# Where a small transpose's copy stands in a step, and which bank takes the last bias columns

## The chip, the cores and the metric

The kernel runs on one core of a Trainium2 chip. Its engines work side by side, each through its own queue in order: TensorE (PE, with PEld for its weight loads) multiplies matrices, VectorE (DVE) and ScalarE (ACT) work on elements and read TensorE's results out of PSUM, GpSimd (POOL) works on elements in SBUF, and SyncE (SP) issues the transfers between DRAM and SBUF. Engines wait for one another by semaphores. The metric is the time of one execution on the device, in microseconds. A profile is one execution with a record of each instruction; its span runs from the first instruction to the last.

## The reference, cut to what matters

Attention over 2 batches, 8 heads, 576 positions and 64 dimensions a head has a bias that a small network computes from the distance of two positions. Two feed-forward layers follow it.

```
scores = q @ k.T / sqrt(64)                      # per batch and head, 576 x 576
x      = log1p(|i - j|) / log1p(max(i, 1))       # distance seen from query position i
bias   = relu(x @ w1 + b1) @ w2                  # 1 -> 32 -> 8 heads
attn   = softmax(scores + bias) ;  y = attn @ v  # 1152 rows of 512
h      = y @ w_in ;  y2 = (h * clip(h + 3, 0, 6) / 6) @ w_out      # 512 -> 2048 -> 512
out    = ((y2 @ w_a) * (y2 @ w_b)) @ w_out2                        # 512 -> 1536 -> 512
```

For a fixed position i the bias depends only on |i - j|, so there are at most 576 distances for each i, and a row of the bias is a row of distances read forward and, for the keys before i, reversed.

## The kernel before, in words

**Steps.** The attention stage is a loop of 36 steps, n = 0 to 35 (line 426). A step handles a tile of 128 queries and a pair of heads u = 0, 1. The scores (L299) are 12 matmuls in three groups of four: K and Q are split into a high and a low part, and each group adds one product. They land in two PSUM tiles `sc` of two banks, one tile for each head of the pair; each bank holds 288 keys, so columns 288 to 511 of every bank stay free. On DVE one reduction a head (L304) adds the bias row, and keeps the minimum of the negated row; ACT takes the exponential with its sum (L308). DVE makes the denominators and their reciprocals (L312, L316), and POOL scales the probabilities (L321).

**Transposes.** Probabilities `P` are transposed one step later. The 64 tail keys of both heads, 128 columns in all, go first (L331), into free columns of the first bank of this step's first score tile, and DVE copies them out (L332). The other 1024 columns take eight transposes (L341) into two banks `tp`; ACT copies the first bank (L343), DVE the second (L345). Yet a step later the product with V follows (L359 for the tail keys, L363), into `pvb`, which is split into a high part (ACT, L372) and a low one (DVE, L378). The next step's scores go into the same two `sc` tiles again, so they wait until the reductions and the copy of the tail keys have read them. From step 27 on the tail keys' transpose uses a bank of its own (`tpb`), and ACT copies it.

**Bias.** While step n runs, it also prepares the bias of a slice g = n + 10 of 16 query positions, up to slice 35 in step 25. Four relus make the hidden layer for g + 1 (`bias_relu`: j = 0, 1, 2 on DVE at L194, j = 3 on ACT at L196). Four matmuls with 32 output rows each (L210) turn that for g into 8 heads of bias over the distances, in one PSUM bank `bps` that exists once. These are copied into an SBUF row `E`, forward and reversed (L216, L218, L225, L227), and SyncE writes E to a DRAM scratch (L239). Eight slices make a block of 128 query positions, which is loaded back as the bias tile of later steps (L259). A slice has 304 to 576 distances. Up to 512 fit one bank; above that, in steps 22 to 25, the distances are halved, and both halves pass through `bps` one after the other.

**Order.** The schedule is written out by hand: each engine runs its instructions in the order of the code, and the framework adds the semaphore waits. In steps 22 to 25 `bias_parts` is a generator that stops between the halves, so that the first half's matmuls stand right behind the scores and its copies ahead of the relus.

**After the steps** come the feed-forward layers, with `_Weights` preparing the weights. Their first three loads (L935) are issued in step 27, behind the last bias loads in SyncE's queue; from step 28 on POOL rescales the first weights (L946) between its normalisations.

Of the kernel before, what the change touches and what calls it, by code (L numbers as in the profile page):

```python
# [8 lines left out]
F32 = mybir.dt.float32  # L9
F32R = mybir.dt.float32r  # L10
AF = mybir.ActivationFunctionType
ALU = mybir.AluOpType
# [9 lines left out]
NSET = S // 16  # L22
NSTEP = 36
LEAD = 2
# [26 lines left out]
def kernel(ctx, tc, cons, qm, qt, kt, vm, vt, wm, out):  # L51
# [8 lines left out]
    V, A, G, T, SP = nc.vector, nc.scalar, nc.gpsimd, nc.tensor, nc.sync  # L60
# [10 lines left out]
    ps = tc.alloc_tile_pool(name="ps", bufs=1, space=PSUM, side="right", reuse_waits="tile")  # L71
    psc0 = tc.alloc_tile_pool(name="psc0", bufs=1, space=PSUM, side="left", reuse_waits="tile")
# [12 lines left out]
    cst3 = ph.tile([128, 1], F32, name="cst3")  # L85
    RELU = "VVVA"
# [45 lines left out]
    sc_tiles = {}  # L132
# [44 lines left out]
    def bias_geom(s):  # L177
        i0 = 16 * s
        R = i0 + 15
        return i0, R, max(R, S - 1 - i0) + 1  # L180

    def bias_relu(s, only=None):

        i0, R, Dd = bias_geom(s)
        if s not in h_tiles:
            h_tiles[s] = [ph.tile([128, S], F32, tag="h", bufs=8, name="ht") for _ in range(4)]
        for j in range(4):
            kind = RELU[j]
            if only is not None and kind not in only:
                continue  # L190
            ht = h_tiles[s][j]
            sc = scl[:, 4 * s + j : 4 * s + j + 1]
            if kind == "V":
                V.tensor_scalar(ht[:, :Dd], ltab[:, :Dd], scalar1=sc, scalar2=negb, op0=ALU.mult, op1=ALU.max)  # L194
            else:
                A.activation(ht[:, :Dd], ltab[:, :Dd], AF.Relu, bias=b1c, scale=sc)  # L196

    def bias_parts(s, rev, wide=False):

        i0, R, Dd = bias_geom(s)  # L200
        hs = h_tiles.pop(s)
        n = 1 if Dd <= 512 else 2
        step = Dd // n
        E = ph.tile([128, S + 16], F32, tag="E", bufs=4, name="E")

        def mm(c):
            bp = psc0.tile([128, 512], F32, tag="w", bufs=4, name="bpw") if wide else ps.tile([128, 512], F32, tag="b", name="bps")
            d0, d1 = c * step, Dd if c == n - 1 else (c + 1) * step
            for j in range(4):
                T.matmul(bp[32 * j : 32 * j + 32, : d1 - d0], w2b, hs[j][:, d0:d1], start=True, stop=True)  # L210
            return bp, d0, d1

        def leave(c, bp, d0, d1):
            f1 = min(d1, S - i0)
            if f1 > d0 and not wide and n > 1 and c == 0:
                V.tensor_scalar(E[:, R + d0 : R + f1], bp[:, : f1 - d0], scalar1=8.0, scalar2=cst3[:, 0:1], op0=ALU.mult, op1=ALU.add)  # L216
            elif f1 > d0:
                A.activation(E[:, R + d0 : R + f1], bp[:, : f1 - d0], AF.Identity, bias=cst3[:, 0:1], scale=8.0)  # L218
            r0, r1 = max(d0, 1), min(d1, R + 1)
            if r1 > r0:  # L220
                src = bp[:, r0 - d0 : r1 - d0]
                dst = E[:, R - r1 + 1 : R - r0 + 1]
                dst = bass.AP(dst.tensor, dst.offset + (r1 - r0 - 1), [dst.ap[0], [-1, r1 - r0]])
                if rev is A and (wide or n == 1 or c):
                    A.activation(dst, src, AF.Identity, bias=cst3[:, 0:1], scale=8.0)  # L225
                else:
                    V.tensor_scalar(dst, src, scalar1=8.0, scalar2=cst3[:, 0:1], op0=ALU.mult, op1=ALU.add)  # L227

        if wide:
            for x in [mm(c) for c in range(n)]:  # L230
                leave(0, *x)
        else:
            for c in range(n):
                leave(c, *mm(c))
                if c < n - 1:
                    yield
        it, sl = divmod(s, 8)
        scr = scratch[it]
        SP.dma_start(  # L239
            bass.AP(scr.tensor, scr.offset + PAD + 16 * sl * H * PITCH - 15, [[H * PITCH + 1, 16], [PITCH, H], [1, S + 15]]),  # L240
            E[:, : S + 15],
        )

    def bias_mm(*args, **kwargs):
        for _ in bias_parts(*args, **kwargs):
            pass

    def bias_load(it, half, pairs=None):
        scr = scratch[it]
# [17 lines left out]
    def qk_units(n):  # L267
        tl, p = divmod(n, 4)
        it = tl // 2
        P = pb.tile([128, 2, S], F32, tag="P", bufs=3, name="P")  # L270
        P_tiles[n] = P
        st = pb.tile([128, 4], F32, tag="st", bufs=4, name="st")
        st_tiles[n] = st


        scs = [psc.tile([128, 2, 512], F32, tag="sc", bufs=2, name="sc") for _ in range(2)]
        sc_tiles[n] = scs[0]
        if tl < 8:
            (qh, ql), j = q_tiles[n], 4 * (tl % 2) + p
            mm = [  # L280
                (u, c, slice(0, 128), q_, k_[:, j], x)
                for x, (q_, k_) in enumerate(((qh, KH), (qh, KL), (ql, KH)))
                for c in range(2)
                for u in range(2)
            ]
            last = 2
        else:

            mm = [
                (u, c, slice(64 * b, 64 * b + 64), q_raw[8][:, p], k_[:, 4 * b + p].bitcast(F32), x)  # L290
                for c in range(2)
                for x, k_ in enumerate((KH, KL))
                for b in range(2)
                for u in range(2)
            ]
            last = 1
        for u, c, r, q_, k_, x in mm:
            d = slice(64 * u, 64 * u + 64)
            T.matmul(scs[u][r, c, 0:288], q_[d, r], k_[d, 288 * c : 288 * c + 288], start=x == 0, stop=x == last)  # L299
        for u in range(2):  # L300
            h, sc = 2 * p + u, scs[u]
            bt = bias_tiles[it, p // 2][:, h % 4, :].rearrange("p (c x) -> p c x", c=2)
            Pu = P[:, u, :].rearrange("p (c x) -> p c x", c=2)
            V.tensor_tensor_reduce(  # L304
                out=Pu, in0=sc[:, :, 0:288], in1=bt, scale=-0.125, scalar=3.0e38,
                op0=ALU.add, op1=ALU.min, accum_out=st[:, u : u + 1],
            )
            A.activation(P[:, u, :], P[:, u, :], AF.Exp, bias=st[:, u : u + 1], scale=-1.0, accum_out=st[:, 2 + u : 3 + u])  # L308

    def denominators(n):  # L310
        st = st_tiles[n]
        V.tensor_scalar(st[:, 2:4], st[:, 2:4], scalar1=1e-9, scalar2=None, op0=ALU.add)  # L312
# [10 lines left out]
    def transpose_tail(n):  # L323

        PT_tiles[n] = pb.tile([128, 9, 128], F32, tag="PT", bufs=2, name="PT")
        if n < NSET - 8 - LEAD:

            tp = sc_tiles[n + 1][:, 0, 288 : 288 + 128]
        else:
            tp = ps.tile([128, 512], F32, tag="b", name="tpb")[:, 0:128]  # L330
        T.transpose(tp, P_tiles[n].rearrange("p a n -> p (a n)")[:, 512:640], ident)  # L331
        (V.tensor_copy if n < NSET - 8 - LEAD else A.copy)(PT_tiles[n][:, 8, :], tp)  # L332
# [56 lines left out]
    for s in range(8 + LEAD):  # L389
        if s < 7 + LEAD:  # L390
            bias_relu(s + 1)
        bias_mm(s, V, wide=True)
        if s in (1, 3):
            load_k(2 + s // 2)
        elif s == 5:
            k_hi(1, A)
        elif s == 6:
            k_lo(1, V)
        elif s == 7:
            load_k(4)  # L400
            load_k(5)
            q_hi(0)
        elif s == 8:
            bias_load(0, 0, 0)
            bias_load(0, 0, 1)
            k_hi(0, V)
            q_lo(0)
            k_lo(0, V)
# [17 lines left out]
    for n in range(NSTEP):  # L426
        g = n + 8 + LEAD
# [2 lines left out]
        if n + 2 < 32:  # L430
            q_hi(n + 2)
        qk_units(n)
        rest = bias_parts(g, A) if g < NSET else iter(())
        if g < NSET and bias_geom(g)[2] > 512:
            next(rest)
        if g + 1 < NSET:
            bias_relu(g + 1, only="V")
        if n >= 2:
            pv(n - 2)
            x_hi(n - 2)  # L440
        if n >= 1 and n - 1 >= NSET - 8 - LEAD:
            transpose_tail(n - 1)
        if g + 1 < NSET:
            bias_relu(g + 1, only="A")
        if g < NSET:
            for _ in rest:
                pass
            if g == NSET - 1:
                bias_load(g // 8, 0)
            elif g % 8 == 7:  # L450
                bias_load(g // 8, 0)
# [14 lines left out]
        if n >= NSTEP - 7:  # L466

            ring.join_next()
        denominators(n)
        reciprocals(n)  # L470
        normalise(n)
# [2 lines left out]
        if n + 2 < 32:  # L474
            q_lo(n + 2, G)
        if n >= 1:
            if n - 1 < NSET - 8 - LEAD:
                transpose_tail(n - 1)
            transposes(n - 1)
        if n >= NSTEP - 8:  # L480
            ring.join_next()
# [217 lines left out]
    for ch in range(NCH1):  # L699
        for i in range(3 if ch == 0 else 0, FC):  # L700
            w = first[i] if ch == 0 else ring.take()
# [456 lines left out]
```

## Time and profile before

| | before |
|---|---|
| median of 3 runs | 610.77 us (610.57 to 611.08) |
| profiled execution, whole | 610.01 us |
| its span | 608.2 us |
| PE busy | 591.7 us (97%) |
| DVE busy | 447.2 us (74%) |
| ACT busy | 341.9 us (56%) |
| POOL busy | 228.3 us (38%) |
| granted TensorE clock, mean | 0.994 of full speed |

Busy shares are averages over the whole span. The attention steps take about 28 to 185 us of it, and DVE is busy for close to nine tenths of most of their slices; behind them PE is full. A busy PE can include time in which a matmul that has been started waits for its PSUM tile, so the gaps between PE's groups are read from its weight loads (PEld) and from the timeline. "Idle before, and what ended it" stands in brackets behind a row, where the profile could tell.

### The profile page before, as it was taken

The page shows a single profiled execution, that of the slowest core. Times are in us where ns is not written, and L with a number is a line of the kernel's source. Part 1 is how long each engine was busy: PE and PEld are TensorE (multiplying, and loading weights), DVE is VectorE, ACT ScalarE, POOL GpSimd, SP SyncE. Part 2 cuts the span into 40 slices and gives each one's busy share as a digit, 9 for nine tenths or more (in the row PEclk, how much of TensorE's full clock was granted, in tenths as well). Part 3 has the DMA queues.
Part 4 walks back from the last instruction along what each step waited for, and adds up shares of the span by engine and source line. Part 5 has one row for each costly group of instructions (what it writes and reads, how often), then busy time and mean ns, then how long its engine had stood idle before and what let it go on. Part 6 is the DMA issues. An engine that isn't in the chain of part 4 may idle for free. (4 is left out here: it accounts for less than half of the span.)

```text
span 608.2 us, 13366 instructions
## 1 busy us (share of the span) xinstructions
PE 591.7 (97%) x5306; PEld 521.3 (86%) x5306; DVE 447.2 (74%) x909; ACT 341.9 (56%) x721; POOL 228.3 (38%) x224
## 2 busy tenths in 40 slices
PE   8699999998999999999999999999999999999997
PEld 5267776766778999999999999999989998899986
DVE  6899888887668993897796566968585577947252
ACT  6689888876877754652572353455446543345310
POOL 0055443434665421221212142365326834377200
PEclk9979999999999999999999999999999999999999
DMA  7874727255923444345333211011154212510012
GB/s 252 265 251 134 254 70 247 80 161 164 250 72 107 134 141 140 105 132 146 104 110 110 66 63 36 0 34 37 36 168 144 71 36 65 171 43 1 0 60 96
DMA packets 28877, 69.27 MB, mean 114 GB/s; under 512 B 5392, under 2 KB 5776, under 8 KB 28816
## 3 DMA queue, kind: packets, MB, share of 16 engines
q1 hardware_dynamic: 28672, 68.35, 37.1%
q8 instruction: 41, 0.67, 0.5%
q14 instruction: 20, 0.16, 0.1%
q10 hardware_dynamic: 144, 0.09, 0.0%
HBM read 55.17 MB, written 13.25 MB: 113 GB/s over the span
## 5 line engine op out<-in xcount | busy, mean ns | idle before, releaser
L980 POOL TENSOR_TENSOR slot<-wv,slot 128x512 fp32r<-128x512 f32 x86 | 118.7, 1385 | 220.3 <-ACT slot L979 156.5
L532 PE MATMUL pair<-xx,slot 128*128 128x384 f32 x576 | 101.5, 335 | 0.0
L532 PEld LDWEIGHTS pair<-xx,slot 128*128 128x128 f32 x576 | 99.8, 188 | 0.2
L532 PE MATMUL pair<-gh,slot 128*128 128x384 f32 x384 | 98.6, 336 | 0.0
L321 POOL TENSOR_SCALAR P<-P,st 128x576 f32<-128x576 f32 x72 | 57.1, 806 | 109.1 <-DVE xx L378 71.9
L740 PE MATMUL pair<-xx,slot 128*128 128x288 f32 x576 | 83.2, 296 | 0.5 <-DVE c L774 0.3
L740 PEld LDWEIGHTS pair<-xx,slot 128*128 128x128 f32 x576 | 78.6, 188 | 1.4 <-DVE c L774 0.6
L948 ACT ACTIVATE wv<-raw 128x512 f32<-128x512 f32 x63 | 42.5, 675 | 57.3 <-DMA raw<-in_wm_dram 34.4
L308 ACT ACTIVATE P<-P,st 128x576 f32<-128x576 f32 x72 | 55.3, 769 | 30.5 <-DVE st L304 30.5
L532 PEld LDWEIGHTS pair<-gh,slot 128*128 128x128 f32 x384 | 69.4, 188 | 0.0
L532 PE MATMUL pair<-slot,gh 128*128 128x512 f32 (+1 forms) x224 | 68.1, 387 | 0.0
L304 DVE CUSTOM_DVE_ANT_0 P<-sc,bias 128x576 f32<-128x576 f32 x72 | 51.7, 754 | 19.2 <-PE sc L299 13.0
L532 PE MATMUL pair<-gl,slot 128*128 128x384 f32 x192 | 64.6, 336 | 0.8 <-DVE gl L550 0.8
L740 PE MATMUL pair<-tt,slot 128*128 128x288 f32 x432 | 64.2, 298 | 0.9 <-ACT u L826 0.9
L979 ACT CAST slot<-wv 128x512 fp32r<-128x512 f32 x86 | 53.0, 620 | 18.9 <-PE pair L740 12.8
L740 PEld LDWEIGHTS pair<-tt,slot 128*128 128x128 f32 x432 | 59.1, 188 | 2.7 <-ACT u L826 2.0
L557 ACT ACTIVATE t<-pair,three 128x384 f32<-128x384 f32 x48 | 27.9, 582 | 45.4 <-PE pair L532 45.3
L532 PEld LDWEIGHTS pair<-slot,gh 128*128 128x128 f32 x224 | 41.3, 188 | 8.9 <-DVE part L883 0.3
L194 DVE TENSOR_SCALAR ht<-cs,scl,negb 128x576 f32<-128x576 f32 (+17 forms) x108 | 48.5, 504 | 0.0
L558 DVE SCALAR_TENSOR_TENSOR u<-t,pair 128x384 f32<-128x384 f32 x48 | 26.4, 550 | 24.7 <-ACT t L557 24.4
L957 DVE TENSOR_SCALAR wm<-wv 128x512 uint32<-128x512 uint32 x59 | 40.5, 686 | 4.8 <-ACT wv L948 4.7
L963 DVE SCALAR_TENSOR_TENSOR wv<-raw,wm 128x512 uint32<-128x512 uint32 x59 | 40.5, 686 | 4.0
(111 smaller groups left out, 1012.9 us busy)
## 6 DMA issues: line engine op xcount, KB each, us to landing
raw<-in_wm_dram SPq DMA_DIRECT2D x68, 512.0 KB, 3.6
scr<-E SPq DMA_DIRECT2D x36, 295.5 KB, 3.6
bias<-scr SPq DMA_DIRECT2D x7, 576.0 KB, 4.8
bias<-scr SPq DMA_DIRECT2D x7, 512.0 KB, 5.5
kraw<-in_kt_dram SPq DMA_DIRECT2D x8, 288.0 KB, 4.5
qraw<-in_qm_dram SPq DMA_DIRECT2D x8, 256.0 KB, 4.8
VM<-in_vm_dram SPq DMA_DIRECT2D x2, 1024.0 KB, 6.2
out_dram<-part SPq DMA_DIRECT2D x7, 256.0 KB, 2.0
```

What stands on the lines that cost most here:

```text
L194: V.tensor_scalar(ht[:, :Dd], ltab[:, :Dd], scalar1=sc, scalar2=negb, op0=ALU.mult, op1=ALU.max)
L304: V.tensor_tensor_reduce(out=Pu, in0=sc[:, :, 0:288], in1=bt, scale=-0.125, scalar=3.0e38, op0=ALU.add, op1=ALU.min, accum_out=st[:, u : u ...
L308: A.activation(P[:, u, :], P[:, u, :], AF.Exp, bias=st[:, u : u + 1], scale=-1.0, accum_out=st[:, 2 + u : 3 + u])
L321: G.tensor_scalar(P[:, u, :], P[:, u, :], scalar1=st[:, 2 + u : 3 + u], scalar2=1.0, op0=ALU.mult, op1=ALU.mult)
L532: T.matmul(ps_ap, l, r, start=(i == 0), stop=(i == len(prods) - 1))
L557: A.activation(t, hp, AF.Relu, bias=three[:, 0:1])
L740: T.matmul(pair[:, j, 0:TQ], l, r, start=start and i == 0, stop=i == 5, skip_group_check=not start)
L948: self.nc.scalar.mul(self.u[k], up, 2.0**-112)
L957: V.tensor_scalar(mid, ub, scalar1=3, scalar2=0x7FFFFFFF, op0=ALU.logical_shift_left, op1=ALU.bitwise_and)
L963: V.scalar_tensor_tensor(out=v, in0=self.words(k, 0), scalar=29, in1=mid, op0=ALU.logical_shift_right, op1=ALU.bitwise_or)
L979: nc.scalar.copy(s[:, 0, :], v)
L980: nc.gpsimd.tensor_tensor(out=s[:, 1, :], in0=v, in1=s[:, 0, :].bitcast(F32), op=ALU.subtract)
```

## The change

There are two edits. First, the tail keys' transpose and copy (`transpose_tail`) of steps 1 to 26 are called ahead of the third DVE relu, which itself is now called just ahead of the denominators, and no longer behind the POOL normalisation and the low parts. Second, `bias_mm` replaces the generator: in steps 22 to 25 the first 512 distances go into `bps`, and those from 512 on into the second bank of this step's second score tile, from column 288. All bias matmuls of a step now stand in one place, behind the product with V. In those steps ACT copies the 511 reversed columns, and DVE the forward ones and those of the score bank.

```
-    def bias_parts(s, rev, wide=False):
+    def bias_mm(s, rev, over=None):
...
+            cuts = [0, min(Dd, 512)] + [Dd] * (Dd > 512)
+            banks = [ps.tile([128, 512], F32, tag="b", name="bps")]
+            if Dd > 512:
+                banks.append(over[:, 1, 288:512])
+        for bp, d0, d1 in zip(banks, cuts, cuts[1:]):
             for j in range(4):
                 T.matmul(bp[32 * j : 32 * j + 32, : d1 - d0], w2b, hs[j][:, d0:d1], start=True, stop=True)
...
+            few = rev is A and Dd > 512
+            if f1 > d0:
+                leave(V if few else A, E[:, R + d0 : R + f1], bp[:, : f1 - d0])
...
+                leave(V if few and d0 else rev, dst, bp[:, r0 - d0 : r1 - d0])
...
         qk_units(n)
-        rest = bias_parts(g, A) if g < NSET else iter(())
-        if g < NSET and bias_geom(g)[2] > 512:
-            next(rest)
         if g + 1 < NSET:
-            bias_relu(g + 1, only="V")
+            bias_relu(g + 1, only=(0, 1))
...
         if g + 1 < NSET:
-            bias_relu(g + 1, only="A")
+            bias_relu(g + 1, only=(3,))
         if g < NSET:
-            for _ in rest:
-                pass
+            bias_mm(g, A, sc_tiles[n][1])
...
+        if 1 <= n <= NSET - 8 - LEAD:
+
+            transpose_tail(n - 1)
+        if g + 1 < NSET:
+            bias_relu(g + 1, only=(2,))
         denominators(n)
...
         if n >= 1:
-            if n - 1 < NSET - 8 - LEAD:
-                transpose_tail(n - 1)
             transposes(n - 1)
```

On DVE, a narrow step (step 7, the relus of 304 columns) before; ISA is the reduction of L304 and the reading of its result:

```order
L304 ISA P,st<-sc,bias 128x576
L304 ISA st 128x1
L194 TENSOR_SCALAR ht<-cs,scl,negb 128x304 x3
L312 TENSOR_SCALAR st<-st 128x2
L316 RECIPROCAL st<-st 128x2
L378 TENSOR_TENSOR xx<-pvb,xx 128x128
L332 COPY PT<-sc 128x128
L345 COPY PT<-tp 128x512
```

and the same step on DVE with the change, where the line numbers are its own (L323 is the tail keys' copy, L336 the larger one):

```order
L295 ISA P,st<-sc,bias 128x576
L295 ISA st 128x1
L191 TENSOR_SCALAR ht<-cs,scl,negb 128x304 x2
L323 COPY PT<-sc 128x128
L191 TENSOR_SCALAR ht<-cs,scl,negb 128x304
L303 TENSOR_SCALAR st<-st 128x2
L307 RECIPROCAL st<-st 128x2
L369 TENSOR_TENSOR xx<-pvb,xx 128x128
L336 COPY PT<-tp 128x512
```

The copy has moved from the fifth place behind the reduction to the second; nothing else has changed its order.

On PE, step 22 (a slice of 528 distances) before, from the scores on:

```order
L299 MATMUL sc<-KH,ql 128x288 x4
L210 MATMUL bps<-ht,cs 32x264 x4
L359 MATMUL pvb<-PT,VT 32x128 x4
L363 MATMUL pvb<-PT,VM 32x128 x16
L210 MATMUL bps<-ht,cs 32x264 x4
L331 MATMUL sc<-ident,P 128x128
L341 MATMUL tp<-ident,P 128x128 x8
```

and with the change:

```order
L290 MATMUL sc<-KH,ql 128x288 x4
L350 MATMUL pvb<-PT,VT 32x128 x4
L354 MATMUL pvb<-PT,VM 32x128 x16
L214 MATMUL bps<-ht,cs 32x512 x4
L214 MATMUL sc<-ht,cs 32x16 x4
L322 MATMUL sc<-ident,P 128x128
L332 MATMUL tp<-ident,P 128x128 x8
```

The first half's group has left its place behind the scores, and both groups stand behind the product with V.

## Rows read from the trace of the kernel before

**Rows 1.** The page's head: span, then busy time and share of each engine.
```profile
span 608.2 us, 13366 instructions
...
PE 591.7 (97%) x5306; PEld 521.3 (86%) x5306; DVE 447.2 (74%) x909; ACT 341.9 (56%) x721; POOL 228.3 (38%) x224
```
**Rows 2.** Who ended idle time ahead of L299: releaser, us, times.
```profile
  DVE PT L332: 6.9, 22
```
**Rows 3.** Timeline, step 7: start, us, engine, line, instruction, count, [idle before, releaser].
```profile
59.35 0.76 DVE L304 CUSTOM_DVE_ANT_0 P<-sc,bias 128x576 f32<-128x576 f32 x1 [0.53 <-PE sc L299]
59.44 0.85 PEld L363 LDWEIGHTS pvb<-PT,VM 128*32 128x32 f32 x32
...
60.71 1.13 DVE L194 TENSOR_SCALAR ht<-cs,scl,negb 128x304 f32<-128x304 f32 x3
...
61.16 1.04 PE L341 MATMUL tp<-ident,P 128*128 128x128 f32 x8
...
62.28 0.28 DVE L332 COPY PT<-sc 128x128 f32<-128x128 f32 x1
...
62.62 0.29 PEld L299 LDWEIGHTS sc<-KH,qh 64*128 64x128 f32 x3 [0.31 <-DVE PT L332]
...
63.15 0.58 ACT L343 COPY PT<-tp 128x512 f32<-128x512 f32 x1
...
63.69 0.76 DVE L304 CUSTOM_DVE_ANT_0 P<-sc,bias 128x576 f32<-128x576 f32 x1 [0.52 <-POOL P L321]
63.78 0.85 PEld L363 LDWEIGHTS pvb<-PT,VM 128*32 128x32 f32 x32
```
**Rows 4.** Timeline, step 20 and the start of step 21.
```profile
117.10 0.76 DVE L304 CUSTOM_DVE_ANT_0 P<-sc,bias 128x576 f32<-128x576 f32 x1 [0.53 <-PE sc L299]
117.14 0.89 PEld L363 LDWEIGHTS pvb<-PT,VM 128*32 128x32 f32 x32
...
121.08 0.58 ACT L343 COPY PT<-tp 128x512 f32<-128x512 f32 x1
...
121.72 0.76 DVE L304 CUSTOM_DVE_ANT_0 P<-sc,bias 128x576 f32<-128x576 f32 x1 [0.54 <-PE sc L299]
```
**Rows 5.** Timeline, step 22 and the start of step 23.
```profile
126.36 0.76 DVE L304 CUSTOM_DVE_ANT_0 P<-sc,bias 128x576 f32<-128x576 f32 x1 [0.54 <-PE sc L299]
...
127.92 0.48 DVE L227 TENSOR_SCALAR E<-bps,cst 128x263 f32<-128x263 f32 x1
...
128.55 0.65 PE L210 MATMUL bps<-ht,cs 128*32 128x264 f32 x8 [0.54 <-DVE E L227]
...
131.62 0.76 DVE L304 CUSTOM_DVE_ANT_0 P<-sc,bias 128x576 f32<-128x576 f32 x1 [0.53 <-PE sc L299]
```
**Rows 6.** Timeline, the end of step 26.
```profile
150.54 0.53 PE L299 MATMUL sc<-KH,qh 64*128 64x288 f32 x3 [0.71 <-DVE PT L332]
...
151.62 0.76 DVE L304 CUSTOM_DVE_ANT_0 P<-sc,bias 128x576 f32<-128x576 f32 x1 [0.53 <-PE sc L299]
```
**Rows 7.** Step 13's last copy, its block's loads (issue; landing), step 16's second reduction.
```profile
88.95 0.57 ACT L225 ACTIVATE E<-bps,cst 128x383 f32<-128x383 f32 x1
...
L259 SPq DMA_DIRECT2D bias<-scr x3: 365/463/470, 92.7 to 93.6; - x3
...
bias<-scr SPq DMA_DIRECT2D x1, 64.0 KB, 5.8
...
99.59 0.75 DVE L304 CUSTOM_DVE_ANT_0 P<-sc,bias 128x576 f32<-128x576 f32 x1
```
**Rows 8.** Timeline: step 25's last copy, the last bias loads, the first weights on POOL.
```profile
145.08 0.50 ACT L225 ACTIVATE E<-bps,cst 128x288 f32<-128x288 f32 x1 [0.34 <-PE bps L210]
...
148.68 3.87 SPq L259 DMA_DIRECT2D bias<-scr  x6
...
161.44 0.66 POOL L946 TENSOR_SCALAR wv<-raw 128x512 f32<-128x512 f32 x1 [0.60 <-DMA raw<-in_wm_dram]
162.06 1.93 POOL L321 TENSOR_SCALAR P<-P,st 128x576 f32<-128x576 f32 x2
```

More of the change, by code (lines that the diff above doesn't have):

```diff
@@ L180, in bias_geom, with bias_relu @@
         return i0, R, max(R, S - 1 - i0) + 1
-    def bias_relu(s, only=None):
+    def bias_relu(s, only=range(4)):
         i0, R, Dd = bias_geom(s)
@@ L186, in bias_relu @@
             h_tiles[s] = [ph.tile([128, S], F32, tag="h", bufs=8, name="ht") for _ in range(4)]
[L187 to L190, printed above, removed]
+        for j in only:
             ht = h_tiles[s][j]
             sc = scl[:, 4 * s + j : 4 * s + j + 1]
-            if kind == "V":
+            if RELU[j] == "V":
                 V.tensor_scalar(ht[:, :Dd], ltab[:, :Dd], scalar1=sc, scalar2=negb, op0=ALU.mult, op1=ALU.max)
@@ L196, in bias_relu @@
                 A.activation(ht[:, :Dd], ltab[:, :Dd], AF.Relu, bias=b1c, scale=sc)
-    def bias_parts(s, rev, wide=False):
+    def bias_mm(s, rev, over=None):
         i0, R, Dd = bias_geom(s)
         hs = h_tiles.pop(s)
-        n = 1 if Dd <= 512 else 2
-        step = Dd // n
         E = ph.tile([128, S + 16], F32, tag="E", bufs=4, name="E")
-        def mm(c):
-            bp = psc0.tile([128, 512], F32, tag="w", bufs=4, name="bpw") if wide else ps.tile([128, 512], F32, tag="b", name="bps")
-            d0, d1 = c * step, Dd if c == n - 1 else (c + 1) * step
+        if rev is V:
+            cuts = [0, Dd] if Dd <= 512 else [0, Dd // 2, Dd]
+            banks = [psc0.tile([128, 512], F32, tag="w", bufs=4, name="bpw") for _ in cuts[1:]]
+        else:
+            cuts = [0, min(Dd, 512)] + [Dd] * (Dd > 512)
[3 more added lines that the diff above has]
+        for bp, d0, d1 in zip(banks, cuts, cuts[1:]):
@@ L209, in mm, with leave @@
             for j in range(4):
                 T.matmul(bp[32 * j : 32 * j + 32, : d1 - d0], w2b, hs[j][:, d0:d1], start=True, stop=True)
-            return bp, d0, d1
-        def leave(c, bp, d0, d1):
+        def leave(eng, dst, src):
+            if eng is A:
+                A.activation(dst, src, AF.Identity, bias=cst3[:, 0:1], scale=8.0)
+            else:
+                V.tensor_scalar(dst, src, scalar1=8.0, scalar2=cst3[:, 0:1], op0=ALU.mult, op1=ALU.add)
+        for bp, d0, d1 in zip(banks, cuts, cuts[1:]):
@@ L214, in leave @@
             f1 = min(d1, S - i0)
[L215 to L218, printed above, removed]
+            few = rev is A and Dd > 512
+            if f1 > d0:
+                leave(V if few else A, E[:, R + d0 : R + f1], bp[:, : f1 - d0])
@@ L219, in leave @@
             r0, r1 = max(d0, 1), min(d1, R + 1)
             if r1 > r0:
-                src = bp[:, r0 - d0 : r1 - d0]
                 dst = E[:, R - r1 + 1 : R - r0 + 1]
                 dst = bass.AP(dst.tensor, dst.offset + (r1 - r0 - 1), [dst.ap[0], [-1, r1 - r0]])
[L224 to L236, printed above, removed]
+                leave(V if few and d0 else rev, dst, bp[:, r0 - d0 : r1 - d0])
         it, sl = divmod(s, 8)
@@ L242, in bias_parts @@
         )
-    def bias_mm(*args, **kwargs):
-        for _ in bias_parts(*args, **kwargs):
-            pass
     def bias_load(it, half, pairs=None):
@@ L276, in qk_units @@
         scs = [psc.tile([128, 2, 512], F32, tag="sc", bufs=2, name="sc") for _ in range(2)]
-        sc_tiles[n] = scs[0]
+        sc_tiles[n] = scs
         if tl < 8:
@@ L326, in transpose_tail @@
         if n < NSET - 8 - LEAD:
-            tp = sc_tiles[n + 1][:, 0, 288 : 288 + 128]
+            tp = sc_tiles[n + 1][0][:, 0, 288 : 288 + 128]
         else:
@@ L391 @@
             bias_relu(s + 1)
-        bias_mm(s, V, wide=True)
+        bias_mm(s, V)
         if s in (1, 3):
@@ L443 @@
         if g + 1 < NSET:
-            bias_relu(g + 1, only="A")
+            bias_relu(g + 1, only=(3,))
         if g < NSET:
-            for _ in rest:
-                pass
+            bias_mm(g, A, sc_tiles[n][1])
             if g == NSET - 1:
```

## The prediction

> **What bounds the kernel now.** I read the page's head first [rows 1]: the span is 608.2 us and TensorE (PE) is busy for 97% of it, so the time goes where PE stops. The change touches only the attention stage (steps n = 0 to 35, about 28 to 185 us), so I then asked which releasers end PE's idle time before the score matmuls at L299 [rows 2]: the tail copy at L332 is named 22 times, 6.9 us in all. One of these, in step 26, is 0.71 us [rows 6]; the other 21 average (6.9 - 0.71) / 21 = 0.30 us. The timeline of step 7 shows the mechanism [rows 3]. I count a step from its first score-and-bias reduction (L304) to the next step's. VectorE (DVE) starts it at 59.35, does three relus from 60.71, and reaches the tail copy only at 62.28. PE's eight transposes started at 61.16 and end near 62.20, but the score tile holds the tail keys' transpose until the copy ends, and PE stands 0.31 us. The step takes 63.69 - 59.35 = 4.34 us. DVE then waits 0.53 us for the scores. So the loop is scores, reductions, relus, small operations, tail copy, scores, with some slack on both engines.
>
> A second gate lies just behind it. The probability-value matmuls at L363 of step 8 need the 128x512 copy (L343) that ScalarE (ACT) makes last in step 7. That copy ends at 63.15 + 0.58 = 63.73 and PE loads the first L363 weights at 63.78, 0.05 us later [rows 3]. In step 20 the copy ends at 121.66 [rows 4], also only just ahead of the next step's weights. No idle time is put down to it because the copy of the tail keys has so far been a little later.
>
> **The change, part by part.**
>
> Narrow steps. The transpose itself keeps its place in PE's order; on DVE its copy moves from behind the reciprocals and the L378 subtraction to between the second and third relu. It could start at about 60.71 + 2/3 x 1.13 = 61.46 instead of 62.28, and end before PE's transposes do. PE's 0.30 us go away. Nothing is added: the same relus, copy and small operations follow one another on DVE, and the normalisation on GpSimd (POOL) begins some 0.2 to 0.3 us later in its step, which nobody waits for until the next step's tail transpose.
>
> What is late next is ACT's copy. Two steps close a loop: reduction of step n to the end of its L343 copy, 0.05 us, then L363 of step n+1 to the reduction of step n+2. ACT's part is 63.73 - 59.35 = 4.38 us in step 7 and does not shorten, because ACT runs without a gap from its first exponential. PE's part is 63.69 - 59.44 = 4.25 us, less the 0.30 us that go: 3.95. Two steps take 4.38 + 0.05 + 3.95 = 8.38, so 4.19 each against 4.34: 0.15 us a step [rows 3]. In step 20 the same sum is 4.56 + 0.05 + (121.72 - 117.14 - 0.30 = 4.28) = 8.89, 4.45 each against 4.62: 0.17 [rows 4]. I expect short and long steps to alternate. Bounds for a narrow step are 0 (ACT takes it all) and 0.30 (ACT's gate is not real); I take 0.16, nearest to the rows. It applies to 16 steps, 6 to 21: 2.6 us. Step 3 gains about 0.2. Steps 4 and 5, and those before 3, gain nothing: there DVE also splits K, and it goes into the next reduction without a gap.
>
> Wide steps 22 to 25 (528 to 576 distances). Before, PE must stop between the two halves of the bias distances until DVE has emptied the single bank: 0.54 us in step 22, behind a 0.48 us reversed 263-column copy that DVE does ahead of its relus [rows 5]. Now the first 512 columns go into that bank and the other 16 to 64 into columns 288 to 511 of the second score bank, one after the other. The number of matmuls and of columns is the same, so I take PE's own time as unchanged. The small ones have no row of their own; by the 264-column row [rows 5] a group can cost 0 to 0.65 us, and the half that disappears shrinks the same, so the ends are -0.2 and +0.2 a step. DVE loses the 263-column copy and gets a 16 to 64 column one; no such row is shown, and I take half of the 0.48 us, with 0 and 0.48 as ends. DVE's own bound falls by 0.53 idle plus 0.24, or 0.77; PE's by 0.54 and a piece of the tail-copy wait, together about 0.65. ACT gets a 511-column copy in place of 264 columns, at most 0.25 us more by the 0.50 us row for 288 columns [rows 8], and it had over a microsecond of room in these steps. So 0.65 a step, 2.0 for steps 22 to 24; step 25 has no relus behind it and gains PE's 0.5. DVE now waits in order for the bias matmuls before the tail copy; queued behind are the third relu and the softmax denominators, and DVE gets there only after two relus, about when PE is done.
>
> Step 26 has no relus at all. PE stood 0.71 us for the tail copy, which waited for the softmax sums on ACT; now it follows the reductions. DVE's idle time of 0.53 us there and the copy's 0.28 us allow the same [rows 6]. I take 0.7.
>
> Together 2.6 + 0.2 + 2.0 + 0.5 + 0.7 = 6.0 us. Two transfers do not get faster with it.
>
> First, the bias rows' round trip through DRAM. Step 13's last piece leaves ACT at 88.95 + 0.57 = 89.52; the third load is issued at 93.6 and lands 5.8 us later, at 99.4; the odd head's reduction of step 16 reads it at 99.59 [rows 7]. Only 0.2 us are free while three steps would gain 0.5. I subtract 0.2. The Trainium skill (DMA: Bandwidth & Descriptors, section "Anatomy of one DMA — SWDGE (gpsimd) path") gives a DMA about 2 us fixed, mostly for the receipt of the write, plus its bytes at 436 GB/s; for 64 KB that would be an estimated 2.2 us, this subtraction would vanish and the gain be 0.2 us larger. The row's 5.8 us, on another path and behind two larger loads, disagrees, and it decides.
>
> Second, the first MoE weights. Their loads stand in SyncE's queue behind the last bias loads, which start at 148.68 after step 25's piece left ACT at 145.58 and was written, and take 3.87 us to issue. POOL already waits 0.60 us for the second weight at 161.44, and the normalisation of step 29 starts the moment that piece of work ends, at 162.06 [rows 8]. That chain moves with step 25's ACT copy, perhaps 0.25 us more than the steps before it, and not with the rest of steps 25 and 26. So of their 1.2 us about 1.0 is given back as a longer POOL wait. It may be 0 if the loads land faster in a quieter moment.
>
> 6.0 - 0.2 - 1.0 = 4.8; I round to 5. Behind step 35 PE is full, and nothing there is edited, so the gain reaches the end. The profiled execution took 610.01 us, which gives 605; the median of the runs shown is 0.76 us higher, 610.77, which gives 605.8, and that is the prediction.
>
> **Rivals.** (a) ACT's gate and the weights' wait do not bind as I say, and every narrow step gets back the full 0.30 us: 17 x 0.30 + 3.2 = 8.3 us, 602.5. For it: no row shows idle time before L363. Against: the 0.05 us between the copy and the weights in step 8. The DMA figure above would push the same way, worth 0.2 us by itself.
>
> (b) Only the wide steps and step 26 pay: ACT's copy, or the DVE copy standing in line for the tail transpose, takes the narrow steps' gain back. 3.2 - 1.0 = 2.2 us, 608.6. For it: both gates are within 0.1 us of each other in step 7.
>
> (c) The copy's new place doesn't release the score tile (a later DVE instruction turns out to be the one waited for), and the bank split is hidden: no change, 610.8. Against: PE's idle time names exactly the copy.
>
> (d) Slower. DVE works in order, and the copy now waits for PE's tail transpose with the third relu, the denominators and the 128x512 copy behind it. If ACT's gate delays L363 by y, the copy waits y minus about 0.2 us; DVE's idle 0.53 us absorbs that until y is about 0.75 us. My sums make y at most 0.3 (in the long steps of the alternation). Were it 0.85, each of about 20 steps would be 0.1 us longer than now: 2 us, 612.8.
>
> **How the numbers follow.** My forecast has a chance of 0.55, with its own range from 604.5 to 607.4; (a) 0.15, (b) 0.16, (c) 0.08, (d) 0.06. The range 602.2 to 609.2 takes in forecast, (a) and (b), which leaves out 0.14, and the unknown costs: four wide steps at 0.2 us either way, narrow steps between 0 and 0.30. About 0.2%, 1.2 us, is what a measurement of this kernel can tell from no change. Faster by more than that: 0.55 + 0.15 + 0.16 = 0.86; within it 0.08; slower 0.06.
>
> **What would show it.** Right: the tail copy no longer ends PE's waits before L299; steps 6 to 21 alternate between about 4.05 and 4.35 us; L363 starts within 0.1 us of the end of ACT's copy in every second step; steps 22 to 24 take about 4.6 us instead of, in step 22, 5.26 [rows 5]; POOL's wait for the first weights grows to 1 us or more. Wrong: narrow steps all near 4.04 (a) or 4.34 (b); a DVE wait in front of the tail copy of over 0.5 us (d); a weight stage that ends no earlier although step 35 does.

## The result, and the profile after

| | before | after |
|---|---|---|
| median of 4 runs each | 610.67 us (610.32 to 611.08) | 605.14 us (604.29 to 605.62) |
| ratio, 95% interval | | 0.9908 (0.9891 to 0.9925) |
| profiled execution, its span | 610.01, 608.2 us | 604.7, 602.9 us |
| granted TensorE clock, mean | 0.994 | 0.994 |

The kernel became 0.92% faster; 605.8 us had been forecast. The head of the page after answers to [rows 1]: the span lost 5.3 us and PE's busy time 6.6 us, while DVE, ACT and POOL are busy for as long as before, to within 0.4 us.

```profile
span 602.9 us, 13362 instructions
...
PE 585.1 (97%) x5306; PEld 516.6 (86%) x5306; DVE 446.9 (74%) x909; ACT 342.3 (57%) x721; POOL 227.9 (38%) x224
```

Who ended PE's idle time ahead of the scores (L290 now) answers to [rows 2]: the tail copy (L323 now) is named twice instead of 22 times, and 0.3 us are left of 6.9.

```profile
  DVE PT L323: 0.3, 2
```

In the list of waits (us in total, times, longest) two new ones stand in its place: PE's weight loads wait for ACT's 128x512 copy ahead of the product with V (L354, formerly L363; most of these waits are listed once more under the matmuls, 3.7 us), and DVE waits for PE's tail transpose.

```profile
PEld pvb L354 <- ACT PT L334: 7.2, 13, 0.8
...
DVE PT L323 <- PE sc L322: 2.6, 9, 0.4
```

The period of a step runs from its first reduction to the next step's. Added up by stage from the two timelines:

| steps | before | after | gained | predicted |
|---|---|---|---|---|
| 0 to 2 | 13.44 | 13.59 | -0.15 | 0 |
| 3 to 5 | 13.13 | 13.28 | -0.15 | 0.2 |
| 6 to 21 | 71.35 | 68.70 | 2.65 | 2.6 - 0.2 |
| 22 to 24 | 15.81 | 13.19 | 2.62 | 2.0 |
| 25 to 28 | 16.54 | 15.04 | 1.50 | 1.2 |
| 29 | 3.86 | 4.64 | -0.78 | -1.0 |
| 30 to 33 | 17.11 | 17.10 | 0.01 | 0 |
| sum | 151.24 | 145.54 | 5.70 | 4.8 |

Step 0 began 0.42 us later in the profiled execution of after (28.86 against 28.44), so that step 34 starts 5.28 us earlier, and that reaches the end. In the executions profiled here step 0 starts anywhere from 27.80 to 29.30 us, so one span alone separates kernels no finer than about a microsecond, while step periods that wait for no load repeat to a few hundredths.

The timeline of steps 7 and 8 answers to [rows 3] (start, us, engine, line, instruction, count, idle before and releaser).

```profile
59.52 0.58 ACT L334 COPY PT<-tp 128x512 f32<-128x512 f32 x1
59.60 0.76 DVE L295 CUSTOM_DVE_ANT_0 P<-sc,bias 128x576 f32<-128x576 f32 x1
...
60.16 0.81 PEld L354 LDWEIGHTS pvb<-PT,VM 128*32 128x32 f32 x32 [0.61 <-ACT PT L334]
...
62.05 0.29 DVE L323 COPY PT<-sc 128x128 f32<-128x128 f32 x1 [0.30 <-PE sc L322]
...
63.41 0.58 ACT L334 COPY PT<-tp 128x512 f32<-128x512 f32 x1
...
63.99 0.76 DVE L295 CUSTOM_DVE_ANT_0 P<-sc,bias 128x576 f32<-128x576 f32 x1 [0.24 <-POOL P L312]
64.04 0.81 PEld L354 LDWEIGHTS pvb<-PT,VM 128*32 128x32 f32 x32
...
67.90 0.76 DVE L295 CUSTOM_DVE_ANT_0 P<-sc,bias 128x576 f32<-128x576 f32 x1
```

ACT's copy of step 6 ends at 60.10 and the first V weights load at 60.16, after 0.61 us of idle: the gate that was hidden by 0.05 us is now in the open. Everything in step 7 comes later for it, and DVE stands 0.30 us in line for the tail transpose. In step 8 the copy ends at 63.99, when the step begins, and no wait for it is recorded. Step 7 takes 4.39 us and step 8 3.91, in place of 4.34 each. The forecast of alternating steps holds, with 0.48 us between a long step and a short one where 0.30 had been forecast. So it does in step 20, which answers to [rows 4]: 4.19 and 4.61 us.

```profile
115.63 0.76 DVE L295 CUSTOM_DVE_ANT_0 P<-sc,bias 128x576 f32<-128x576 f32 x1 [0.17 <-POOL P L312]
...
119.82 0.76 DVE L295 CUSTOM_DVE_ANT_0 P<-sc,bias 128x576 f32<-128x576 f32 x1
...
120.24 0.81 PEld L354 LDWEIGHTS pvb<-PT,VM 128*32 128x32 f32 x32 [0.47 <-ACT PT L334]
```

Step 22 answers to [rows 5]:

```profile
124.43 0.76 DVE L295 CUSTOM_DVE_ANT_0 P<-sc,bias 128x576 f32<-128x576 f32 x1
...
126.94 0.23 DVE L220 TENSOR_SCALAR E<-sc,cst 128x16 f32<-128x16 f32 x1
127.08 0.28 DVE L323 COPY PT<-sc 128x128 f32<-128x128 f32 x1
...
128.21 0.68 DVE L336 COPY PT<-tp 128x512 f32<-128x512 f32 x1
...
128.81 0.75 DVE L295 CUSTOM_DVE_ANT_0 P<-sc,bias 128x576 f32<-128x576 f32 x1
```

It takes 4.38 us against 5.26, and DVE has no idle time ahead of 128.81. The 16-column copy takes 0.23 us. In the view by stretches (length, then busy us of PE, PEld, DVE, ACT and POOL with their counts, granted clock, DMA share, GB/s) DVE is busy for 4.34 of the 4.38 us, so it is the bound now:

```profile
124.43:128.81 4.38, 4.38 (x85) 3.23 (x77) 4.34 (x14) 3.73 (x10) 1.69 (x4) 1.00 0.37 80
```
The end of step 26 answers to [rows 6]: the scores have lost their wait, and the step takes 3.53 instead of 4.35 us.

```profile
144.21 0.53 PE L290 MATMUL sc<-KH,qh 64*128 64x288 f32 x4
...
145.58 0.75 DVE L295 CUSTOM_DVE_ANT_0 P<-sc,bias 128x576 f32<-128x576 f32 x1
```

Two waits took part of it back. The second reduction of step 16 [rows 7] now stands 0.48 us (it is put down to PE here; an experiment below shows that it waits for the bias load), and POOL stands 0.94 and 0.63 us for the first weights, so that the normalisation of step 29 begins at 156.82 [rows 8].

```profile
99.00 0.76 DVE L295 CUSTOM_DVE_ANT_0 P<-sc,bias 128x576 f32<-128x576 f32 x1 [0.48 <-PE pvb L354]
...
154.91 0.64 POOL L936 TENSOR_SCALAR wv<-raw 128x512 f32<-128x512 f32 x1 [0.94 <-DMA raw<-in_wm_dram]
156.19 0.65 POOL L936 TENSOR_SCALAR wv<-raw 128x512 f32<-128x512 f32 x1 [0.63 <-DMA raw<-in_wm_dram]
156.82 1.90 POOL L312 TENSOR_SCALAR P<-P,st 128x576 f32<-128x576 f32 x2
```

### The profile page after: what moved, and what is told of

Read it like the earlier page. It is cut to its first block, busy times and chain, and to the rows that moved or that the text cites. A ratio compares the mean times of both kernels' runs of the same rounds, so it can differ in the third digit from the quotient of the medians.

```text
span 602.9 us, 13362 instructions
## 1 busy us (share of the span) xinstructions
PE 585.1 (97%) x5306; PEld 516.6 (86%) x5306; DVE 446.9 (74%) x909; ACT 342.3 (57%) x721; POOL 227.9 (38%) x224
## 5 line engine op out<-in xcount | busy, mean ns | idle before, releaser
L299 ACT ACTIVATE P<-P,st 128x576 f32<-128x576 f32 x72 | 55.3, 770 | 25.2 <-DVE st L295 24.8
L191 DVE TENSOR_SCALAR ht<-cs,scl,negb 128x576 f32<-128x576 f32 (+17 forms) x108 | 50.4, 504 | 0.0
L354 PE MATMUL pvb<-PT,VM 128*32 128x128 f32 (+1 forms) x1280 | 40.2, 264 | 3.8 <-ACT PT L334 3.7
```

Of the source, the lines that this page charges most:

```text
L354: T.matmul(pvb[32 * w : 32 * w + 32, p, c0:c1], VM[:, k, b * H + 2 * p + u, d], PT[:, 4 * u + k, c0:c1], start=False, stop=(k == 3),)
```

## The experiments

Ratios are against the kernel before, with 95% intervals. The first four kernels ran on one chip and the last four on another, each beside new runs of the kernel before (medians 610.52 and 610.29 us), so they are compared by their ratios and by their steps; after has 0.9908 (0.9891 to 0.9925). Line numbers are each kernel's own.

**The first edit alone.** On the kernel before:

```
-            bias_relu(g + 1, only="V")
+            bias_relu(g + 1, only=(0, 1))
...
+        if 1 <= n <= NSET - 8 - LEAD:
+            transpose_tail(n - 1)
+        if g + 1 < NSET:
+            bias_relu(g + 1, only=(2,))
```

> The first edit alone: the tail copy goes between the relus, the bias distances of the wide steps still pass through one bank in halves. My account: steps 6 to 21 as with the whole change, 68.7 us in all against 71.35 before (-2.6), step 26 near 3.5 (-0.8), but the wide steps 22 to 24 stay near 5.1 (-0.15 each), since PE still waits about half a microsecond for DVE between the halves. With the weights' wait giving the gain of step 26 back: about -3.2 us, 607.5. Rival: the wide steps' gain of 0.87 us each comes from the copy's place as well; then they fall by 0.5 us or more here and the whole is -4.5 us or better, 606.

Measured: 606.8 us, ratio 0.9947 (0.9930 to 0.9963). Steps 6 to 21 take 68.58 us (68.70 with both edits) and step 26 3.53, as with both; step 29 takes 4.68. Steps 22 to 24 take 15.32 us against 15.81. Step 22 of this run:

```profile
123.59 0.76 DVE L302 CUSTOM_DVE_ANT_0 P<-sc,bias 128x576 f32<-128x576 f32 x1 [0.16 <-POOL P L319]
...
125.78 0.65 PE L208 MATMUL bps<-ht,cs 128*32 128x264 f32 x8 [0.66 <-DVE E L225]
...
128.70 0.76 DVE L302 CUSTOM_DVE_ANT_0 P<-sc,bias 128x576 f32<-128x576 f32 x1
```

The tail copy no longer holds PE there, but PE stands 0.66 us for the single bank. So the narrow steps' gain and step 26's belong to the first edit, and so does what is given back in step 29.

**The second edit alone.** `bias_mm` with the score bank; relus and tail copy stay where they were:

```
-            for _ in rest:
-                pass
+            bias_mm(g, A, sc_tiles[n][1])
```

> The second edit alone: the wide steps use the second score bank, the tail copy stays behind the subtraction. My account: narrow steps and step 26 as before; in steps 22 to 24 PE's wait between the halves goes, but the copy still ends about 3.9 us into the step and holds the scores, so only 0.2 us each; step 25, which has no relus, gains 0.5. In all about -1 us, 609.7: the two edits are worth more together than apart. Rival: the edits add, and the wide steps' 3.3 us are the bank split's alone: 607.4.

Measured: 608.9 us, ratio 0.9976 (0.9964 to 0.9988). Narrow steps are unchanged (4.34 us in steps 6 to 9). Steps 22 to 24 take 15.06 us, step 25 4.42, step 29 4.03. Step 22 of this run:

```profile
126.08 0.76 DVE L295 CUSTOM_DVE_ANT_0 P<-sc,bias 128x576 f32<-128x576 f32 x1 [0.53 <-PE sc L290]
...
129.99 0.29 PEld L290 LDWEIGHTS sc<-KH,qh 64*128 64x128 f32 x3 [0.47 <-DVE PT L323]
...
131.08 0.76 DVE L295 CUSTOM_DVE_ANT_0 P<-sc,bias 128x576 f32<-128x576 f32 x1 [0.54 <-PE sc L290]
```

PE no longer stops for the bank; it now stops for the tail copy instead (0.47 us), and DVE still waits 0.54 us for the scores. In steps 22 to 24 the first edit alone gains 0.49 us, the second alone 0.75, both 2.62: each of them uncovers the wait that the other removes.

**ACT's copy earlier.** On the kernel with both edits, in steps 1 to 25 the transposes and ACT's 128x512 copy stand ahead of ACT's copies into E; DVE's copies stay where they are:

```
-            bias_mm(g, A, sc_tiles[n][1])
+            finish = bias_mm(g, A, sc_tiles[n][1], later_copy=early)
+            if early:
+                transpose_tail(n - 1, 0)
+                transposes(n - 1, 0)
+                finish()
```

> With the whole change, and ACT's 128x512 copy of the transposes moved ahead of its copies of the bias row in steps 1 to 25; same work. If ACT's copy is the gate that limits the narrow steps, the alternation of 3.9 and 4.4 us goes and steps without a wait for a load take 4.0 (step 7) to 4.3 us (step 20). But the bias row now leaves ACT about 0.5 us later in each step, so the round trip through DRAM should stop steps 8 and 16 by about 1.1 and 1.3 us, and the first weights come 0.5 us later: the whole within 0.7 us of the changed kernel, near 605.4. Rival: DVE's tail copy waiting in order for PE sets the alternation; then it stays, and the time is 605 to 606.

Measured: 604.52 us, ratio 0.9918 (0.9895 to 0.9940), which is not apart from after; the profiled execution took 607.1 us, the other three 604.2 to 604.7. Steps 6 to 21 take 65.31 us, 3.39 less than with both edits, and the alternation is gone: steps 9 to 15 take 3.93 to 4.03 each. Just ahead of the first reduction of step 12 (79.97) PE loads the V weights without a wait, 0.23 us after ACT's copy has ended:

```profile
79.10 0.56 ACT L351 COPY PT<-tp 128x512 f32<-128x512 f32 x1
...
79.89 0.90 PEld L373 LDWEIGHTS pvb<-PT,VM 128*32 128x32 f32 x32
```

That confirms ACT's gate. The bias rows had been expected to stop steps 8 and 16 by over a microsecond; step 8 takes 4.32 us and step 16 4.56, against 3.91 and 4.46 in after. But little arrives at the end: the E copies end half a microsecond later in their step, and the weights behind the last bias loads come only 1.19 us sooner than in after, while step 29 begins 2.98 us sooner (149.68 against 152.66). POOL waits 2.75 us for the first of them:

```profile
153.72 0.64 POOL L959 TENSOR_SCALAR wv<-raw 128x512 f32<-128x512 f32 x1 [2.75 <-DMA raw<-in_wm_dram]
```

Step 29 takes 6.11 us, step 30 6.60, step 31 5.19. By stretches of this kernel, PE is busy for 3.02 and 2.86 of 5 us, and the granted clock (the third number from the end) falls:

```profile
150.00:155.00 5.00, 3.02 (x51) 2.41 (x43) 1.70 (x7) 2.92 (x8) 1.60 (x3) 1.00 1.04 355
155.00:160.00 5.00, 2.86 (x48) 2.62 (x49) 3.71 (x12) 2.24 (x7) 4.68 (x6) 0.68 1.06 198
160.00:165.00 5.00, 5.00 (x63) 4.10 (x63) 1.53 (x5) 2.72 (x8) 1.16 (x2) 0.64 0.55 122
```

So the gate was there, and in this execution what it had held back was taken by the weights' wait and, in part, by the clock.

**An older bias tile.** With both edits, the first steps of three blocks read the bias tile of the block before, and so wait for no new load:

```
-            bt = bias_tiles[it, p // 2][:, h % 4, :].rearrange("p (c x) -> p c x", c=2)
+            bt = bias_tiles[(it - 1, 1) if n in (8, 16, 24) else (it, p // 2)][:, h % 4, :].rearrange("p (c x) -> p c x", c=2)
```

> With the whole change, but steps 8, 16 and 24 read the bias tile of the block before, which is long loaded, in place of the freshly loaded one (so the values of these steps are not the reference's). If the second reduction of step 16 waits for the third bias load, step 16 falls from 4.46 to about 4.05 and step 17 from 4.67 to about 4.5, and the kernel gains 0.4 to 0.6 us over the changed one, near 604.7. Rival: it waits for something else (the row names a matmul of PE); then step 16 stays at 4.46 and the time at 605.1.

Measured: 604.31 us, ratio 0.9912 (0.9888 to 0.9935); seven of the eight executions took 603.5 to 605.0 us, one 609.56. Step 16 takes 4.07 us instead of 4.46 and step 17 4.56 instead of 4.67; the second reduction of step 16 follows the first without a wait:

```profile
98.92 0.75 DVE L295 CUSTOM_DVE_ANT_0 P<-sc,bias 128x576 f32<-128x576 f32 x1
```

So step 16 waited for the bias load, although the row named PE; with the first edit alone the same place is put down to the load itself (0.35 us at 98.16). Step 29 takes 4.81 instead of 4.64: a part of the half microsecond is given back there. In time, the difference to after is within the intervals.

**Weights' work behind the normalisation.** With both edits, POOL's first two pieces of weight work are issued behind step 29's normalisation:

```
-        if n >= NSTEP - 7:
+        if n >= NSTEP - 6:
...
-        if n >= NSTEP - 8:
+        if n >= NSTEP - 7:
+            ring.join_next()
+        if n in (NSTEP - 7, NSTEP - 6):
```

> The whole change, and POOL's first two pieces of weight work moved from ahead of step 29's normalisation to behind it, with one more piece in step 30 so that the count is caught up. If the wait for the first weights is what makes step 29 4.64 us instead of 3.86, it falls to 3.5 to 3.7 and everything behind comes 1.0 to 1.2 us earlier: 604.0. Rival: step 29 is long for another reason, or the gain is lost again when the weights come late to the MoE stage: 605.1 or more.

Measured: 607.46 us, ratio 0.9955 (0.9941 to 0.9969): slower than after, and the expectation missed. Step 29 takes 6.38 us and step 31 5.68. POOL's normalisation starts 1.66 us earlier than in after (156.82), but DVE works in order, and its first piece of weight work stands ahead of step 30's reduction and waits for POOL's:

```profile
155.16 1.46 POOL L312 TENSOR_SCALAR P<-P,st 128x576 f32<-128x576 f32 x2 [1.73 <-DVE xx L369]
...
157.02 1.29 POOL L937 TENSOR_SCALAR wv<-raw 128x512 f32<-128x512 f32 x2
...
157.71 0.88 DVE L948 TENSOR_SCALAR wv<-wv 128x512 uint32<-128x512 uint32 x1 [2.56 <-POOL wv L937]
158.51 0.74 DVE L295 CUSTOM_DVE_ANT_0 P<-sc,bias 128x576 f32<-128x576 f32 x1
```

The wait was not removed. It moved from POOL to the next engine that takes the weight.

**Weights loaded first.** With both edits, the first three weight loads are issued ahead of the last block's six bias loads:

```
-            if g == NSET - 1:
-                bias_load(g // 8, 0)
-            elif g % 8 == 7:
+            if g % 8 == 7:
...
+            bias_load(4, 0)
```

> The whole change, and the first three weight loads issued ahead of the six bias loads of the last block (which only step 32 reads), same work. My account: the weights land about 4 us earlier, POOL does not wait, the normalisation of step 29 starts near 155.6 instead of 156.8 us, so 1.1 us less: 604.0. Rival: the loads share the same transfers and the bias tile comes late to step 32 instead: 605 or more.

Measured: 603.73 us, ratio 0.9894 (0.9877 to 0.9910). Step 29 takes 3.83 us; POOL does both pieces of weight work without a wait for a DMA, and the normalisation waits for DVE alone.

```profile
153.24 1.29 POOL L935 TENSOR_SCALAR wv<-raw 128x512 f32<-128x512 f32 x2
...
155.29 1.93 POOL L312 TENSOR_SCALAR P<-P,st 128x576 f32<-128x576 f32 x2 [0.76 <-DVE xx L369]
```

Step 32, whose bias tile is now loaded later, takes 4.47 us as before. That is the place in SyncE's queue that the prediction named, and its price is 4.64 - 3.83 = 0.81 us. The times' intervals overlap with those of after; the step's row carries the verdict.

**ACT's copy earlier and the weights first.** Both edits of these two kernels together:

```
+            finish = bias_mm(g, A, sc_tiles[n][1], later_copy=early)
...
+            bias_load(4, 0)
```

> Both cures at once: ACT's 128x512 copy ahead of its bias copies in steps 1 to 25, and the first weight loads ahead of the last bias loads. With ACT's copy first, step 28 began 3 us earlier (counted from step 0), but the weights' wait took it back in steps 29 to 31. If that is all, the two together give 3 + 1 us over the changed kernel: about 601.2. Rival: another wait takes most of it, 603 to 604.5.

Measured: 602.9 us, ratio 0.9884 (0.9867 to 0.9901): less gain than expected and close to the rival, with an interval that still touches that of after. Step 29 takes 3.83 us and steps 30 to 33 take 17.11 again. But blocks now start too early for their bias, and DVE waits for it by up to 0.85 us at a time: step 8 takes 4.33 us, steps 15 and 16 4.80 and 4.76, step 24 5.31. ACT's copies into E come later in the step, and with them each block's loads.

**The same, but for the last slice of a block.** As the kernel just told of, with ACT's old order in steps 5, 13 and 21, whose copies into E complete a block:

```
-            early = n >= 1
+            early = n >= 1 and g % 8 != 7
```

> As both cures at once, but in the steps that finish a block of bias rows (5, 13, 21) ACT keeps the old order, so the block's last row leaves it 0.5 us earlier. If the round trip through DRAM is what makes steps 8 and 16 long (4.3 and 4.6 us instead of about 3.9 and 4.1), each shrinks by up to 0.4 us while steps 6, 14 and 22 pay up to 0.3: between 0.5 us better and the same, 600.8 to 601.2. Rival: those steps are long for another reason: no better, or worse by 0.3 to 0.6 us.

Measured: 601.58 us, ratio 0.9861 (0.9847 to 0.9876), the lowest median of all. Its interval lies apart from that of after, but not from that of the kernel just told of. It lies 0.4 us above the range that had been expected. Step 8 takes 3.95 us and step 24 4.41, and the steps that complete a block pay for it (steps 14 and 22: 4.53 and 4.65 us instead of 4.01 and 4.38). Step 16 still takes 4.95, since its bias has not landed:

```profile
97.36 0.76 DVE L300 CUSTOM_DVE_ANT_0 P<-sc,bias 128x576 f32<-128x576 f32 x1 [0.96 <-DMA bias<-scr]
```

## Why the prediction was right, and where its sizes were off

The places where most of the time is gained and given back are those that were forecast; their sizes were off, and the total is in part luck. Against the terms in the table, steps 0 to 5 brought 0.50 us less and all later ones 1.40 us more, 0.62 of it in the wide steps; the two errors have opposite signs.

**Narrow steps.** The tail copy was what PE waited for, and ACT's copy was next. The runs with the first edit alone and with ACT's copy earlier show both: steps 9 and 10 take 4.00 + 3.93 = 7.93 us with ACT's copy earlier and 4.41 + 3.96 = 8.37 with the gate. A pair of 8.30 us came out in steps 7 and 8 where 8.38 had been summed: from the start of the V weights at 64.04 to the reduction at 67.90 it takes 3.86 us, and not 3.95.

The 0.30 us that were to go from PE's part came out of [rows 2] by a wrong reading. In the list of waits of the kernel before, the weight loads account for 21 of the 22 times:

```profile
PEld sc L299 <- DVE PT L332: 6.2, 21, 0.9
```

The other one, 0.71 us, is the matmul behind the last of them, so step 26 was counted twice, and the other 20 average (6.2 - 0.9) / 20 = 0.26 us. The tail copy cost PE more than that, though, since part of the wait stood inside a matmul already begun. In step 7 before, the scores took 63.60 - 62.13 = 1.47 us from their first weights to the next group's:

```profile
62.13 0.18 PEld L299 LDWEIGHTS sc<-KH,qh 64*128 64x128 f32 x1 [0.17 <-DVE st L312]
...
63.60 0.16 PEld L359 LDWEIGHTS pvb<-PT,VT 128*32 128x32 f32 x8 [0.16 <-issue]
```

and in step 7 of after 63.79 - 62.81 = 0.98:

```profile
62.81 0.30 PEld L290 LDWEIGHTS sc<-KH,qh 64*128 64x128 f32 x4 [0.17 <-DVE st L303]
...
63.79 0.16 PEld L350 LDWEIGHTS pvb<-PT,VT 128*32 128x32 f32 x8 [0.17 <-DVE PT L336]
```

The fourth rival's y, the delay of the V weights by ACT's gate, had been put at 0.3 us at most. In step 7 of after the weights stand 0.61 us and the tail copy behind them 0.30. DVE still had 0.24 us of idle time ahead of the next reduction (63.99), in place of 0.52 before, so its slack took the delay up, with less to spare than the prediction had said.

**Bias round trip.** 0.2 us had been subtracted; by the run with an older bias tile it is 0.39 in step 16 and 0.11 in step 17. Steps 6 to 21 take 68.24 us there, 3.11 less than before, or 0.19 a step instead of 0.16; the two errors nearly cancelled. The landing also varies: step 16 took 4.33 us with the first edit alone, 4.91 with the second alone, which had gained nothing before it. The Trainium skill (DMA: Bandwidth & Descriptors, section "Anatomy of one DMA — SWDGE (gpsimd) path") has a fit for another path than SyncE's; taken for this one, it gives an estimated 2.2 us for the 64 KB load, and this wait would have vanished. Those loads took a median of 5.1 us in the trace of after, and the wait is there.

**Steps 3 to 5.** The step of the argument that failed is that steps 4 and 5 lose nothing. Step 3 gained 0.34, more than the 0.2 forecast, but step 4 lost 0.42. In step 4 of after:

```profile
46.91 0.81 PEld L354 LDWEIGHTS pvb<-PT,VM 128*32 128x32 f32 x32 [0.50 <-ACT PT L334]
...
48.88 0.29 DVE L323 COPY PT<-sc 128x128 f32<-128x128 f32 x1 [0.24 <-PE sc L322]
...
50.51 0.85 DVE L169 TENSOR_TENSOR KL<-kraw,KH 128x576 fp32r<-128x576 f32 x1
```

ACT's gate delays PE by half a microsecond, the copy then stands 0.24 us in DVE's line for the transpose, and DVE has no idle time here to absorb it, since it splits K as well; the split itself takes 0.85 us instead of 0.75. This is the mechanism of the fourth rival, in the one place where DVE had no slack. The first edit alone has the same step (4.84 us). With ACT's copy earlier the step still takes 4.85: ACT converts K in this step too (0.67 us, KH), and DVE then waits 0.26 us for the softmax sums instead. So the 0.24 us are read from the row, and no run shows that the step shortens when the gate goes; why the split takes longer stays open.

**Wide steps.** Forecast 0.65 a step as the smaller of PE's and DVE's shares; measured 0.87 to 0.88. PE's share was too small. Its scores took 131.52 - 130.26 = 1.26 us from their first weights to the next group in step 22 before, and 128.47 - 127.49 = 0.98 after, so the tail copy cost 0.28 us there and not the 0.11 that were taken. DVE set the step at last: from the start of its E copy to the next instruction 0.14 us instead of 0.40, and from that of its 128x512 copy to the next reduction 0.60 instead of 1.22; together 0.88. The 0.24 us for the smaller copy was right (0.26). The rows of before, beside those of [rows 5]:

```profile
128.32 1.50 DVE L194 TENSOR_SCALAR ht<-cs,scl,negb 128x544 f32<-128x544 f32 x3
...
130.40 0.68 DVE L345 COPY PT<-tp 128x512 f32<-128x512 f32 x1
```

ACT's copy of 511 columns took 0.67 us where that of 264 had taken 0.46. The "at most 0.25" of the prediction held, but it does not follow from its one row, which in proportion to the columns gives 0.43.

**Steps 25, 26 and the weights.** 0.67 and 0.82 us were gained where 0.5 and 0.7 had been forecast, and 0.78 of the forecast 1.0 was given back by the weights' wait. The weights-first run shows that this wait is the position in SyncE's queue, and the second edit alone, which leaves step 26 at 4.35 us, gives back only 0.17.

Of the rivals, the first (no gate, 602.5) is near what the kernel with ACT's copy earlier and the weights first comes to, 602.9; the second is refuted by the narrow steps with the first edit alone, the third by the 0.3 us that are left of the tail copy's 6.9; the fourth is real in step 4 only. The edits' single gains, 2.74 and 0.90 us in steps 0 to 33, make 3.64 and not 5.70; of the difference 1.38 lies in steps 22 to 24, the rest in steps 0 to 2, 16 and 29, of which the last two wait for loads.

## What to carry to other kernels

A gate that ends 0.05 us ahead of the one removed shows no idle time; work out from the timeline when every other input of the same instruction, and of those behind it in the loop, is ready, since the second gate sets the size of the gain. Two waits in one loop that hide one another pay in full only when both go, so a trial of one edit alone says little of the pair. Before an early stage is made faster, look up the transfers whose issue does not move with it: here the bias tiles and the first weights took back what came early, and placing the transfer earlier in its queue paid, while moving its consumer behind other work only moved the wait.

## What the runs showed of the hardware that was not expected

In the profiled run with ACT's copy earlier the granted clock was 1.00 up to 155 us and 0.68 and 0.64 in the next two stretches of 5 us: partly at 1.2 and partly at 2.4 GHz. PE had stood idle for about 2 us in the stretch ahead of them. Eight transposes' weight loads took 1.72 us there against 0.91 at full clock:

```profile
158.50 1.72 PEld L349 LDWEIGHTS tp<-ident,P 128*128 128x128 f32 x8
```

In the run with the weights' work late it was 0.70 from 160 to 165 us. The kernel before has the same pair of figures in step 1: the granted clock is 0.50 from 33 to 36 us, and the eight loads that begin at 33.98 take 1.72 us. So part of the price of a long wait on POOL can be paid on PE after the wait is over; how much of the time it made up was not measured by itself.
